# GpSimd instructions wait for the VectorE work that stands ahead of them on the shared port in the scheduler's order

## The chip, the cores and the metric

One Trainium2 chip, one of its cores. The metric is the device time of one execution in microseconds (us). The kernel before takes 637.94 us in the median of three runs (637.08 to 638.41).

## The reference

Causal attention over 4 batches and 12 heads of 448 tokens with 64 features, and behind it a feed-forward layer over all 1792 tokens:

```python
scores = scale * np.matmul(q, k.transpose(0, 1, 3, 2))
scores = np.where(mask, -1000000000.0, scores)
attn = np.exp(scores - np.max(scores, axis=-1, keepdims=True))
attn = attn / (np.sum(attn, axis=-1, keepdims=True) + 1e-09)
attn_out = np.matmul(attn, v)
x = np.ascontiguousarray(attn_out.transpose(0, 2, 1, 3)).reshape(B * S, H * D)
h = x @ w_in                              # 1792x768 by 768x2048
g = h * np.clip(h + 3.0, 0.0, 6.0) / 6.0
out = g @ w_out                           # 1792x2048 by 2048x768
```

All inputs and the output are float32.

## The kernel before

The 1792 tokens are done in four groups of 448 (`S`). Group 0 holds the first 112 rows of every batch, groups 1 to 3 the later ones, cut so that each has 448 rows. `first_pair` computes the attention of group 0 and `unit` that of groups 1 to 3, for one pair of heads at a time. `group` runs the feed-forward layer for groups 0 and 1; groups 2 and 3 share one layer (`last_x`, `last_sums`, `last_first`, `last_second`) that works on sums and differences of blocks with seven products in place of eight.

Float32 products are made of three passes on TensorE: each operand is cut into a high part, rounded to a format of fewer bits (`float32r`), and the rest, and `triple` (lines 674 to 676) multiplies high by high, high by low and low by high. The cutting is what most of the other engines' work is: ScalarE makes the high part (`move`, line 274; tiles `wh`, `gh`), and VectorE or GpSimd subtracts it (`minus`, line 286; tiles `wl`, `gl`, `kl`). The attention has besides, in `unit`: the mask and the row maximum on VectorE (line 561), the exponential on ScalarE (line 568), the inverse of the row sums on VectorE (lines 580 and 581), the scaling of the rows by it on VectorE or GpSimd (line 588; tiles `pr` of 112x224 and 112x336, and a `d` tile of 112x448), the transposes of the scaled rows on TensorE (line 600), and the product with v (line 529).

The order of the work is no fixed program. All steps are first recorded as `Op`s in a `Flow` with a key (roughly the time at which a step is due), the engines that may do it and their relative cost, and the tiles it touches. `Flow.run` then goes through them as a list scheduler with its own idea of durations, gives each to an engine and a time, and returns a list that is sorted by time. At the end of the kernel each entry is emitted in that order, so every engine gets its instructions in the scheduler's order, and the framework adds the semaphore waits that the data need.

The scheduler knows a port that VectorE and GpSimd share. Each `Op` has a set `port` (line 66): GpSimd always, and VectorE only where no tile of the `Op` lies in PSUM. In `run`, an `Op` whose engine is in its `port` does not start while `self.port`, the time until which the port is taken, lies ahead. So in the plan no VectorE `Op` of that kind and no GpSimd `Op` lie beside each other. Before the change nothing in the program holds the chip to that: each of the two engines starts an instruction as soon as its data are there. A few short VectorE steps are recorded with `port=False` (the inverse on lines 580 and 581 is one) and are outside the rule.

Of the kernel before, what the change touches and what calls it, by code (L numbers as in the profile page):

```python
# [16 lines left out]
B, H, S, D = 4, 12, 448, 64  # L17
# [51 lines left out]
class Flow:  # L69
# [119 lines left out]
    def start(self, o, e, now, need, out, busy, post):  # L189
        for t, n in need.items():  # L190
            self.free[t] -= n
        for b in o.bufs:
            b.held = True
        t, o.ends = now, []
        if e == "PE" and o.tiled != self.mode:
            t += self.SWITCH / 2
            self.mode = o.tiled
        for d, emit, _ in o.parts:
            out.append((t, len(out), e, emit))
            t += d * o.ways[e][0]  # L200
            if o.nbytes:
                self.dma = max(self.dma, t) + o.nbytes / self.DMA_RATE
                o.ends.append(self.dma + self.DMA_LATENCY)
            else:
                o.ends.append(t)
        busy[e] = t
        if e in o.port:
            self.port = t
        post(t, "idle", None)
        post(o.ends[-1], "end", o)  # L210
        for a, i in o.then:
            a.waits -= 1
            a.ready = max(a.ready, o.ends[i] + (0 if o.nbytes or e == "PE" and list(a.ways) == [e] else self.TAIL if list(a.ways) == [e] else self.LATENCY))
            if not a.waits:
                post(max(a.ready, now), "ready", a)
# [3 lines left out]
def tile_causal_attention_hardswish_moe(ctx: ExitStack, tc: tile.TileContext, q, k, v, w_in, w_out, out):  # L219
    nc = tc.nc  # L220
# [42 lines left out]
    def dma(key, nbytes, o, i, r=(), w=(), queue="SP"):  # L263
        start = nc.sync.dma_start if queue == "SP" else nc.scalar.dma_start
        flow.op(key, {queue: (1, 0)}, [(0.1, lambda e: start(out=o(), in_=i()), w)], r, nbytes=nbytes)
# [30 lines left out]
    def setup():  # L296
        nc.vector.memset(ident, 1.0)
        nc.vector.memset(mask, 0.0)
        nc.vector.memset(three, 3.0)
        nc.gpsimd.affine_select(  # L300
            out=ident, in_=ident, pattern=[[-1, C]], base=0, channel_multiplier=1,
            compare_op=ALU.is_equal, fill=0.0,
        )
        nc.gpsimd.affine_select(
            out=mask[:, R:], in_=mask[:, R:], pattern=[[-1, C]], base=0, channel_multiplier=1,
            compare_op=ALU.is_ge, fill=-8.0e9,
        )
        nc.vector.tensor_copy(identr, ident)
        nc.vector.tensor_copy(maskr, mask[:, R:].unsqueeze(1).to_broadcast([C, B, C]))
# [361 lines left out]
    def triple(ps, n, wh, wl, c, xh, xl, start, stop, more=False):  # L671

        a = slice(128 * c, 128 * c + 128)
        nc.tensor.matmul(ps, ap(wh)[:, a], xh, start=start, stop=False, skip_group_check=more)  # L674
        nc.tensor.matmul(ps, ap(wh)[:, a], xl, start=False, stop=False, skip_group_check=more)  # L675
        nc.tensor.matmul(ps, ap(wl)[:, a], xh, start=False, stop=stop, skip_group_check=more)  # L676
# [377 lines left out]
    last_second(last_first(last_x()))  # L1054
    order = flow.run()
    setup()
    with tc.manual_schedule():
        for _, _, e, emit in order:
            emit(e)


# [34 lines left out]
```

## Time and profile before

| | |
|---|---|
| median of three runs | 637.94 us (637.08 to 638.41) |
| profiled execution, its own time | 639.0 us |
| its span, first to last instruction | 637.3 us |
| mean granted TensorE clock | 0.991 |
| TensorE matmul busy | 609.3 us, 96% of the span |
| VectorE busy | 530.8 us, 83% |
| ScalarE busy | 372.1 us, 58% |
| GpSimd busy | 248.4 us, 39% |

The engines are PE (TensorE; PEld is its weight load), DVE (VectorE), ACT (ScalarE), POOL (GpSimd) and SP (the queue that issues most transfers). Of a matmul the profile shows a modelled end, and matmuls overlap. "Idle before" is the time in which an engine did nothing in front of an instruction, with what released it behind the arrow. An instruction that an engine has begun and that cannot go on, because another engine has a resource, is shown as a longer instruction and not as idle time.

### The profile page before, as it was taken

The numbers are of one execution on the slowest core, as the hardware profiler recorded it, in microseconds if no ns is written. First come the engines' busy times: TensorE is split into PE (matmuls) and PEld (weight loads), VectorE is DVE, ScalarE is ACT, GpSimd is POOL, SyncE is SP. The second block draws the span as 40 slices with busy tenths as digits, with TensorE's granted clock in tenths as the row PEclk, the third lists the DMA queues.
The fourth block names the chain that finished last, engine by engine and source line by source line (L and its number), as shares of the span: only waits on it lengthen the run. The fifth ranks groups of instructions, "written<-read, shape, count | busy, mean of one in ns | idle before, by whom it ended". The sixth has DMA issues, their size and how long they took to land. (4 is left out here: it accounts for less than half of the span.)

```text
span 637.3 us, 11372 instructions
## 1 busy us (share of the span) xinstructions
PE 609.3 (96%) x3636; PEld 529.9 (83%) x3636; DVE 530.8 (83%) x1130; ACT 372.1 (58%) x865; POOL 248.4 (39%) x248
## 2 busy tenths in 40 slices
PE   7789989999999999899998999999999999999997
PEld 5569769788778888778777888898999999999996
DVE  4799999879787889978998798389999899999561
ACT  3866656655456777567566656365545566555530
POOL 1666657455455454545555243003411045030000
PEclk9979999999999999989999999999999999999999
DMA  9978878779877865645556764445434545774421
GB/s 210 257 252 281 277 227 239 274 210 288 284 237 236 269 201 164 202 130 153 144 153 180 216 183 126 140 137 164 160 106 144 198 147 172 233 241 126 122 70 61
DMA packets 86139, 121.35 MB, mean 190 GB/s; under 512 B 22784, under 2 KB 61888, under 8 KB 86080
## 3 DMA queue, kind: packets, MB, share of 16 engines
q1 hardware_dynamic: 85648, 120.45, 62.4%
q8 instruction: 29, 0.48, 0.3%
q14 instruction: 30, 0.25, 0.1%
q10 hardware_dynamic: 432, 0.17, 0.1%
HBM read 93.45 MB, written 27.13 MB: 189 GB/s over the span
## 5 line engine op out<-in xcount | busy, mean ns | idle before, releaser
L674 PE MATMUL b<-d,wh 128*128 128x448 f32 x504 | 187.5, 372 | 1.9 <-DVE vr L286 1.6
L676 PE MATMUL b<-d,wl 128*128 128x448 f32 x504 | 183.0, 363 | 0.0
L675 PE MATMUL b<-d,wh 128*128 128x448 f32 x504 | 182.1, 361 | 0.0
L274 ACT CAST wh<-wd 128x768 fp32r<-128x768 f32 (+1 forms) x92 | 71.7, 780 | 62.5 <-PE b L675 50.8
L674 PEld LDWEIGHTS b<-d,wh 128*128 128x128 f32 x504 | 94.7, 188 | 10.6 <-DVE vr L286 2.8
L286 DVE TENSOR_TENSOR wl<-wd,wh 128x768 fp32r<-128x768 f32 (+1 forms) x79 | 76.1, 963 | 31.7 <-ACT wh L274 29.6
L676 PEld LDWEIGHTS b<-d,wl 128*128 128x128 f32 x504 | 94.6, 188 | 7.0
L675 PEld LDWEIGHTS b<-d,wh 128*128 128x128 f32 x504 | 94.6, 188 | 5.9
L561 DVE CUSTOM_DVE_ANT_0 b<-b,mask 112x448 f32<-112x448 f32 (+2 forms) x144 | 69.5, 534 | 19.2 <-PE b L506 12.6
L286 POOL TENSOR_TENSOR wl<-d,wh 128x512 fp32r<-128x512 f32 (+1 forms) x40 | 61.3, 1532 | 43.9 <-ACT wh L274 36.3
L674 PE MATMUL b<-gh,wh 128*128 128x448 f32 x192 | 73.8, 384 | 1.4 <-DVE d L277 1.1
L676 PE MATMUL b<-gh,wl 128*128 128x448 f32 x192 | 69.8, 363 | 0.0
L675 PE MATMUL b<-gl,wh 128*128 128x448 f32 x192 | 69.6, 362 | 0.0
L274 ACT COPY d<-b 112x336 f32<-112x336 f32 (+3 forms) x122 | 51.5, 452 | 28.9 <-PE b L600 23.5
L286 POOL TENSOR_TENSOR wd<-wd 128x256 f32<-128x256 f32 (+1 forms) x13 | 13.7, 1054 | 95.3 <-DVE wl L286 46.6
L568 ACT ACTIVATE pr<-b,prow 112x336 f32<-112x336 f32 (+1 forms) x96 | 46.8, 496 | 6.5 <-DVE prow L561 3.0
L600 PE MATMUL b<-ident,pr 112*112 112x112 f32 x240 | 44.1, 263 | 5.0 <-ACT pr L568 2.4
L588 POOL TENSOR_SCALAR pr<-pr,prow 112x224 f32<-112x224 f32 (+1 forms) x55 | 30.1, 558 | 47.4 <-DVE prow L581 40.5
L529 PE MATMUL b<-d,vr 112*64 112x224 f32 (+2 forms) x504 | 46.0, 334 | 0.0
L529 PEld LDWEIGHTS b<-d,vr 112*64 112x64 f32 x504 | 31.1, 139 | 15.5 <-issue 2.6
L274 ACT CAST wh<-d 128x512 fp32r<-128x512 f32 (+1 forms) x40 | 28.3, 708 | 24.5 <-DVE d L653 16.4
L568 ACT ACTIVATE d<-b,prow 112x448 f32<-112x448 f32 x48 | 30.2, 635 | 21.1 <-DVE prow L561 16.1
(115 smaller groups left out, 1191.4 us busy)
## 6 DMA issues: line engine op xcount, KB each, us to landing
wd<-in_w_in_dram SPq DMA_DIRECT2D x32, 384.0 KB, 5.6
wd<-in_w_out_dram SPq DMA_DIRECT2D x24, 512.0 KB, 5.4
wd<-kept_w SPq DMA_DIRECT2D x32, 384.0 KB, 3.7
wd<-kept_w SPq DMA_DIRECT2D x84, 128.0 KB, 3.2
d<-in_k_dram SPq DMA_DIRECT2D x80, 112.0 KB, 2.7
kept_w<-d SPq DMA_DIRECT2D x16, 384.0 KB, 6.4
kept_w<-d SPq DMA_DIRECT2D x24, 256.0 KB, 5.3
wd<-kept_w SPq DMA_DIRECT2D x24, 256.0 KB, 2.9
```

What stands on the lines that cost most here:

```text
L274: nc.scalar.copy(o(), i()) if scale is None else nc.scalar.mul(o(), i(), scale)
L286: (nc.gpsimd if e == "P" else nc.vector).tensor_tensor(o(), a(), b(), op)
L529: nc.tensor.matmul(ap(av)[64 * e:64 * e + 64, off + nq - w:off + nq], ap(vr)[:, j, e, :], ap(ph)[:, e, o:o + w], start=(j == 0), stop=(j = ...
L561: lambda _, e=e, i=i, w=w, dst=dst, st=st: nc.vector.tensor_tensor_reduce(dst(), dst(), mask[:, S - w:], -0.125, 3.0e38, ALU.add, ALU.min, ...
L568: lambda _, e=e, i=i, dst=dst, st=st, pr=pr: nc.scalar.activation(row_of(pr, e, i), dst(), ACTF.Exp, bias=ap(st)[:, e, i:i + 1], scale=-1. ...
L588: (nc.gpsimd if w == "P" else nc.vector).tensor_scalar(x, x, ap(st)[:, e, 4 + i:5 + i], 1.0, ALU.mult, ALU.mult)
L600: nc.tensor.transpose(ap(tp)[:C, C * o:C * o + C], row_of(pr, e, i)[:, C * j:C * j + C], ident)
L674: nc.tensor.matmul(ps, ap(wh)[:, a], xh, start=start, stop=False, skip_group_check=more)
L675: nc.tensor.matmul(ps, ap(wh)[:, a], xl, start=False, stop=False, skip_group_check=more)
L676: nc.tensor.matmul(ps, ap(wl)[:, a], xh, start=False, stop=stop, skip_group_check=more)
```

## The change

`Flow.start` hands each instruction's `port` on with its entry, and the loop that emits keeps the last instruction of a VectorE `Op` that uses the port (`older`). The next GpSimd instruction in the list gets a dependency on it, as though it read what that instruction writes, and `older` is cleared, so that one GpSimd instruction waits and those behind it in GpSimd's own queue come after it anyway. VectorE gets no wait on GpSimd.

```diff
-            out.append((t, len(out), e, emit))
+            out.append((t, len(out), e, emit, o.port))
...
+
+    sync = mybir.DependencyInfo(mybir.DependencyClass.Sync, mybir.DependencyReason.DATA)
+    older = None
     with tc.manual_schedule():
-        for _, _, e, emit in order:
+        for _, _, e, emit, port in order:
+            traced = nc.cur_bb.bb.instructions
+            n = len(traced)
             emit(e)
+            if e == "D" and "D" in port:
+                older = traced[-1].name
+            elif e == "P" and older:
+                tc.add_manual_dep(traced[n], older, sync, reason="port")
+                older = None
```

The plan is the same, and no engine's instructions change places. 73 of GpSimd's 242 tensor instructions get the new dependency. Where the data made such an instruction wait for VectorE already, the wait is now for a later point of VectorE's work; where not, a wait is new. In the listings below `DVE_49` and the like are the semaphores by which an engine tells how far it has come.

The first place is GpSimd's queue in group 0's feed-forward layer, where `gl` is the low part of a hidden row and `wl` that of a weight; after them stands the scaling of a short row of the next attention unit:

```order
 L286 TENSOR_TENSOR gl<-r,gh 128x448 [waits Activation_49]
 L588 TENSOR_SCALAR pr_993<-pr_993,prow 112x224 [waits DVE_49]
-L286 TENSOR_TENSOR gl<-r,gh 128x448 [waits Activation_49]
+L286 TENSOR_TENSOR gl<-r,gh 128x448 [waits DVE_49,Activation_49]
 L286 TENSOR_TENSOR wl<-d,wh 128x768 [waits PE_49,Pool_49]
 L588 TENSOR_SCALAR pr_1005<-pr_1005,prow 112x224 [waits DVE_49]
```

The second `gl` waited for ScalarE's high part alone and now waits for VectorE too; the `wl` behind it has no wait of its own for VectorE and comes after it. The same pattern stands once more, one unit later.

The second place is GpSimd's queue in group 1's feed-forward layer, two weights' low parts and the scaling of a row behind them:

```order
 L286 TENSOR_TENSOR wl<-wd,wh 128x768 [waits PE_49,Activation_49,Pool_49]
-L286 TENSOR_TENSOR wl<-wd,wh 128x768 [waits PE_49,Activation_49]
+L286 TENSOR_TENSOR wl<-wd,wh 128x768 [waits DVE_49,PE_49,Activation_49]
 L588 TENSOR_SCALAR pr_3425<-pr_3425,prow 112x224 [waits DVE_49]
 L588 TENSOR_SCALAR pr_3468<-pr_3468,prow 112x336
```

The first `wl` starts as before, the second one only after VectorE.

The third place is a little later in the same layer, where GpSimd scales two full rows:

```order
 L286 TENSOR_TENSOR wl<-wd,wh 128x768 [waits PE_49,Activation_49]
-L588 TENSOR_SCALAR d<-d,prow 112x448 x2
+L588 TENSOR_SCALAR d<-d,prow 112x448 [waits DVE_49]
+L588 TENSOR_SCALAR d<-d,prow 112x448
 L588 TENSOR_SCALAR pr_3921<-pr_3921,prow 112x224 [waits DVE_49,Activation_49]
```

The first of the two rows now waits for VectorE, where before it came straight behind the `wl`.

## Rows read from the trace of the kernel before

**Rows 1.** Windows: length, busy of PE, PEld, DVE, ACT, POOL, PEclk, DMA, GB/s.

```profile
210.00:425.00 215.00, 206.81 (x1372) 178.39 (x1371) 179.93 (x428) 138.69 (x346) 89.88 (x101) 0.99 0.58 169
425.00:637.30 212.30, 206.88 (x1030) 192.31 (x1028) 177.46 (x287) 107.67 (x181) 39.14 (x29) 1.00 0.48 150
```

**Rows 2.** TensorE's waits from 45 us on: us in total, times, longest us.

```profile
PE b L600 <- DVE d L588: 3.9, 5, 1.5
PE b L600 <- ACT pr L568: 2.4, 2, 1.8
PE b L674 <- DVE vr L286: 1.6, 2, 1.5
PE b L600 <- POOL pr L588: 1.5, 1, 1.5
PE b L508 <- DVE d L286: 1.3, 4, 0.5
PE b L674 <- DVE d L277: 1.1, 1, 1.1
PE b L600 <- DVE pr L588: 1.0, 1, 1.0
```

**Rows 3.** Line 588 on VectorE, full rows: ns min/median/max, first and last start.

```profile
L588 DVE TENSOR_SCALAR d<-d,prow x30: 433/446/2048, 52.8 to 394.9; 112x448 f32<-112x448 f32 x30
```

**Rows 4.** Timeline, 82 to 90 us, GpSimd, VectorE, TensorE: start, us, engine, instruction [idle before <-releaser].

```profile
82.65 1.22 POOL L286 TENSOR_TENSOR gl<-r,gh 128x448 fp32r<-128x448 f32 x1 [0.58 <-ACT gh L274]
83.82 1.95 POOL L286 TENSOR_TENSOR wl<-d,wh 128x768 fp32r<-128x768 f32 x1
89.18 0.88 POOL L588 TENSOR_SCALAR pr<-pr,prow 112x224 f32<-112x224 f32 x2 [3.41 <-DVE prow L581]
...
82.53 1.52 DVE L588 TENSOR_SCALAR pr<-pr,prow 112x224 f32<-112x224 f32 x2
83.97 2.05 DVE L588 TENSOR_SCALAR d<-d,prow 112x448 f32<-112x448 f32 x1
...
86.08 0.31 PE L600 MATMUL b<-ident,d 112*112 112x112 f32 x1 [0.25 <-DVE d L588]
89.68 0.41 PE L600 MATMUL b<-ident,pr 112*112 112x112 f32 x2 [1.50 <-POOL pr L588]
```

**Rows 5.** Timeline, 110 to 114 us, the same three engines.

```profile
111.17 1.91 POOL L286 TENSOR_TENSOR wl<-d,wh 128x768 fp32r<-128x768 f32 x1
...
111.32 2.01 DVE L588 TENSOR_SCALAR d<-d,prow 112x448 f32<-112x448 f32 x1
...
113.39 0.31 PE L600 MATMUL b<-ident,d 112*112 112x112 f32 x1 [1.38 <-DVE d L588]
```

**Rows 6.** Timeline, 263 to 270 us, the same.

```profile
267.78 1.81 POOL L286 TENSOR_TENSOR wl<-wd,wh 128x768 fp32r<-128x768 f32 x1 [2.69 <-ACT wh L274]
...
263.55 1.57 DVE L580 TENSOR_SCALAR prow<-prow 112x4 f32<-112x4 f32 x1
...
267.85 2.00 DVE L588 TENSOR_SCALAR d<-d,prow 112x448 f32<-112x448 f32 x1
...
269.90 0.31 PE L600 MATMUL b<-ident,d 112*112 112x112 f32 x1 [1.54 <-DVE d L588]
```

**Rows 7.** Timeline, 301 to 304 us, the same.

```profile
301.65 2.21 POOL L588 TENSOR_SCALAR d<-d,prow 112x448 f32<-112x448 f32 x2
...
302.73 0.70 DVE L286 TENSOR_TENSOR d<-d 64x112 fp32r<-64x112 f32 x2
...
303.30 0.45 PE L600 MATMUL b<-ident,d 112*112 112x112 f32 x3
```

**Rows 8.** Timeline, 568 to 596 us: GpSimd, VectorE, ScalarE.

```profile
568.49 1.81 POOL L286 TENSOR_TENSOR gh<-gl,gh 128x448 f32<-128x448 f32 x1 [3.57 <-DVE gh L286]
...
578.34 1.15 DVE L286 TENSOR_TENSOR gh<-gl,gh 128x448 f32<-128x448 f32 x2
...
594.50 1.03 ACT L274 CAST d<-gh 128x448 fp32r<-128x448 f32 x2
```

## The prediction

> **What bounds the kernel now.** Start with the windows by stage: from 210 us to the end TensorE is busy for 206.81 of 215.00 and 206.88 of 212.30 us, VectorE for 179.93 and 177.46, GpSimd for 89.88 and 39.14 [rows 1]. TensorE sets the time, and the most that a change on other engines can return is TensorE's idle time. Next, what ends that idle time. From 45 us on, the list of TensorE's waits has seven entries of 1.0 us or more, in sum 12.8 us [rows 2]. Four of them (3.9, 1.5, 1.3 and 1.0) end on an instruction of VectorE or GpSimd that works between tiles in SBUF and so counts as a user of the shared port in the scheduler; `vr` (1.6) and the copy of line 277 (1.1) read a PSUM bank, and 2.4 us end on ScalarE. About 13 us is the ceiling for this change, and the 7.7 us of the four are what it acts on directly.
>
> Then the form of those instructions. The scaling of a full row on VectorE takes 433 ns at least and 446 in the median of 30, but 2048 at most [rows 3]. The timeline shows what lies beside the long ones. At 83.97 us it takes 2.05 us while GpSimd has a `wl` of 1.95 us, begun 0.15 us before [rows 4]; at 111.32 us 2.01 us beside a `wl` begun 0.15 us before [rows 5]; at 267.85 us 2.00 us beside one begun 0.07 us before [rows 6]. Each ends about 0.25 us after GpSimd's, so nearly all of its own 0.44 us is done once GpSimd has let go: one engine has the port and the other stands. The Trainium skill (SBUF — State Buffer, the section on the two separate sides) calls the pair of ports an exclusive lock that whichever of the two starts first holds for its whole instruction; these three rows agree.
>
> **What the change adds.** It moves nothing on any engine and removes nothing. 73 GpSimd instructions get a dependency on VectorE. Laid against the trace (start of each, against the end of the VectorE instruction that it is to wait for), 14 started after that end anyway and 59 started before it: 5 before 210 us, 33 from there to 425, 21 behind. Their lateness is 136 us in sum, from 0.02 to 11.0 us; the longest is the `gh` at 568.49 us, which is to wait for the second of the two at 578.34 [rows 8]. What is paid in GpSimd's time is no path by itself: it is idle for 125 us in the one stage and 173 in the other [rows 1]. A wait that now ends on VectorE costs about 0.1 us more by itself (TensorE started 0.05 us after the VectorE instruction that released it [rows 6]); 59 of these are 6 us of that idle time. No SP transfer is moved; some wait for a buffer that GpSimd frees later.
>
> **The terms.** First, group 0's layer. With the change the `gl` at 82.65 and the `wl` at 83.82 stand back until the VectorE rows are done. These are two short rows, together 1.52 us where 0.33 us each would do without GpSimd, so 0.9 too long, and the full row, 1.6 us too long [rows 4]. VectorE is 2.5 us earlier. TensorE's 0.25 us at 86.08 go, and at 89.68 so do the 1.50 us in front of a row that GpSimd scales: it had waited 3.41 us for the inverse, which stands in VectorE's queue behind the long rows [rows 4]. **−1.75 us.**
>
> Second, the same one unit later: 1.38 us in front of 113.39 go [rows 5]. **−1.4 us.** Third, group 1: the `wl` at 267.78 will wait for two more pairs of scaled rows, the full row ends at 268.3 instead of 269.85, and 1.54 us in front of 269.90 go [rows 6]. **−1.5 us.** The condition is the same in all three: what GpSimd makes there must have slack. The low parts `wl` and `gl` are made for products that the plan has ahead, and neither stands in TensorE's list as a wait on GpSimd [rows 2]; the one with the longest lateness, 11.0 us, is ready at 570.30 and read by ScalarE in the pair at 594.50 [rows 8]. I take it that the others have slack too, the more so as VectorE ends earlier than in the old trace.
>
> Fourth, the small ones: the rest of the first line (3.9 − 0.25 − 1.38 − 1.54 = 0.7 us) and the four waits of the score products for a `d` of line 286 (1.3 us) [rows 2]. Not each has a GpSimd instruction beside it that the change moves; between 0 and −2.0 I take −1.3.
>
> Fifth, the waits that end on ScalarE, on the copies and on `vr` (2.4, 1.1, 1.6) and the one for `pr` (1.0) [rows 2], 6.1 us. Those end on work that stands behind VectorE's queue, so a freer VectorE may shorten them; but behind them may be a transfer or TensorE itself. Between 0 and −6.1 I take −1.6, a quarter, nearer to the lower end, because none of the first three is a user of the port itself.
>
> Sixth, a loss that can be read off: at 301.65 GpSimd scales two full rows in 2.21 us and TensorE takes the first at 303.30 without idle time [rows 7]. With the change the first waits for the last of the VectorE pair that now ends at 303.43. Two instructions of about 0.65 us in place of the 2.21 end at 304.1 for the first, so TensorE is up to 0.8 us late, less what VectorE gains there: **+0.6 us**.
>
> Sum: −1.75 − 1.4 − 1.5 − 1.3 − 1.6 + 0.6 = −6.95, rounded to −7.0 us. The profiled execution took 639.0 us, 1.1 above the median of 637.94; it becomes 632.0, and the median **631.0 us**.
>
> **A rule against it.** The rows say that a GpSimd instruction that waits for the port loses nothing that TensorE needs. If the port is simply an exclusive lock, what one engine gains the other loses, and the sum of both stays. The Trainium skill has the exclusive lock (the section named above) and advises in Perfetto Trace Analysis (on the GPSIMD instruction) to treat a GpSimd span in a profile as unreliable. By these the order would be worth nothing of its own, and my reading of who held the port would be soft: that is the first rival below, 637.5 us. What speaks against it is VectorE's own rows: 2.05 for 0.44 us, three times, each with TensorE idle behind it [rows 4 to 6].
>
> **The rivals.** (a) *The wait only changes hands.* VectorE is faster, but TensorE's idle time is then ended by ScalarE, a transfer, or a GpSimd row, in the same places. For it: 2.4 us already end on ScalarE [rows 2]. Against it: the three big terms are waits for exactly the stretched row. It gives 0 to −1.3 us: 637.5 us. That the new waits are held already by other semaphores, so that the program does the same, falls here too; the listings show new ones at all three places. (b) *Half of it*: the three big terms come, the rest is paid back by GpSimd rows that are late: −2 to −3.5 us, about 635. (c) *Slower*: in group 1's stage, 33 GpSimd starts move back, and among these are the low parts `kl` of keys and the scaled rows, whose readers, score products and transposes, stand close behind. The place is the sixth term; its price is 0.6 to 0.8 us each. It decides when more than one in three of the 33 is late for TensorE: 14 of them at 0.75 us are +10, which with −7 makes +3: 641 us. Against it: VectorE ends earlier there, and TensorE's list has a single entry on GpSimd so far [rows 2].
>
> **The numbers.** My forecast has 0.68 (628 to 634), half of it 0.12, no gain 0.10, slower 0.10. By 0.2% (1.3 us), about what a measurement can tell from no change: faster 0.80, same 0.10, slower 0.10. The low end takes most of the fifth term's 6.1 and the fourth's 2.0 without the sixth: −4.65 − 2.0 − 4.3 = −11, 627 us; the high end takes in half the gain and part of the first rival: 637. By one case alone it would be 628 to 634.
>
> **What would show it.** Right: no full row of line 588 on VectorE above about 1 us in groups 0 and 1; the entry for `d` of line 588 in TensorE's list down from 3.9 to below 1.0; GpSimd's idle time ended far more often by VectorE. The inverse on line 580 stays stretched in places (1.57 us at 263.55 [rows 6]), since the scheduler does not count it as a user of the port. Wrong: new entries in TensorE's list on GpSimd's `kl`, `wl` or `pr` of more than 2 us in sum, or `d` of line 588 still at 3 us with another instruction beside it.

## The result and the profile after

The changed kernel takes 628.46 us in the median of 4 runs (627.74 to 628.89), the kernel before 638.17 on the same chip (637.08 to 638.47): a ratio of 0.985 [0.9833, 0.9867], or −9.7 us. The forecast was 631.0 with a range of 627 to 637, and faster. The sign, the range and the mechanism hold; the size was 2.7 us short.

The profiled execution took 628.89 us, 10.1 less than the one of before. The head of its page, with the span and each engine's busy time:

```profile
span 627.2 us, 11383 instructions
...
PE 604.6 (96%) x3636; PEld 530.0 (85%) x3636; DVE 515.1 (82%) x1130; ACT 373.1 (59%) x865; POOL 234.4 (37%) x248
```

VectorE was busy for 530.8 us before and GpSimd for 248.4. **Both are shorter**, by 15.7 and 14.0 us, with the same count of instructions. An instruction that stands at the shared port counts as busy, so the page of before held these waits as work. GpSimd now waits on a semaphore instead, which the profile shows as idle time. TensorE's waits from 45 us on (us in total, times, longest), which answer to [rows 2]:

```profile
PE b L600 <- ACT pr L568: 4.3, 2, 3.7
PE b L600 <- DVE pr L588: 0.8, 1, 0.8
PE b L600 <- POOL d L588: 0.5, 1, 0.5
PE b L674 <- DVE d L653: 0.3, 1, 0.3
PE b L508 <- ACT d L274: 0.2, 1, 0.2
```

Five of the seven entries are gone, all but the two for `pr` that end on ScalarE and VectorE: the 3.9 us for `d` of line 588, 1.6 for `vr`, 1.5 for GpSimd's `pr`, 1.3 for `d` of line 286, and 1.1 for the copy of line 277. One has grown, that on ScalarE, from 2.4 to 4.3 us. The two groups of VectorE's lines (ns least, median, longest), the first of which answers to [rows 3]:

```profile
L588 DVE TENSOR_SCALAR d<-d,prow x30: 434/445/664, 52.5 to 386.6; 112x448 f32<-112x448 f32 x30
L580 DVE TENSOR_SCALAR prow<-prow x36: 158/286/1833, 46.7 to 383.4; 112x6 f32<-112x6 f32 x12, 112x2 f32<-112x2 f32 x12, 112x4 f32<-112x4 f32 x12
```

The longest full row took 2048 ns and now takes 664. The inverse on line 580, which the scheduler does not count as a user of the port, is stretched more than before. Of the kernel before:

```profile
L580 DVE TENSOR_SCALAR prow<-prow x36: 152/165/1572, 47.0 to 391.9; 112x6 f32<-112x6 f32 x12, 112x2 f32<-112x2 f32 x12, 112x4 f32<-112x4 f32 x12
```

Group 0's layer, which answers to [rows 4] (start, us, engine, instruction, idle time before it and its end):

```profile
82.72 0.44 DVE L588 TENSOR_SCALAR d<-d,prow 112x448 f32<-112x448 f32 x1
...
83.31 1.15 POOL L286 TENSOR_TENSOR gl<-r,gh 128x448 fp32r<-128x448 f32 x1 [1.61 <-PE b L600]
...
84.41 1.86 POOL L286 TENSOR_TENSOR wl<-d,wh 128x768 fp32r<-128x768 f32 x1
...
86.61 0.89 POOL L588 TENSOR_SCALAR pr<-pr,prow 112x224 f32<-112x224 f32 x2 [0.33 <-DVE prow L581]
...
85.11 0.35 PE L600 MATMUL b<-ident,pr 112*112 112x112 f32 x2
85.31 0.26 PE L600 MATMUL b<-ident,d 112*112 112x112 f32 x1
...
87.21 0.35 PE L600 MATMUL b<-ident,pr 112*112 112x112 f32 x2
```

GpSimd's `gl` starts 0.15 us after the full row has ended at 83.16, and the `wl` comes behind it. The full row takes 0.44 us where it took 2.05, and neither of TensorE's rows at 85.31 and 87.21 has idle time before it. (The releaser named for `gl` is the event that came last by the profile; the semaphore that the change added is VectorE's.) The second and the third place, which answer to [rows 5] and [rows 6], look the same:

```profile
107.90 0.44 DVE L588 TENSOR_SCALAR d<-d,prow 112x448 f32<-112x448 f32 x1
...
109.59 1.86 POOL L286 TENSOR_TENSOR wl<-d,wh 128x768 fp32r<-128x768 f32 x1
...
262.26 0.44 DVE L588 TENSOR_SCALAR d<-d,prow 112x448 f32<-112x448 f32 x1
...
263.54 1.83 POOL L286 TENSOR_TENSOR wl<-wd,wh 128x768 fp32r<-128x768 f32 x1 [1.99 <-DVE d L588]
```

And the place of the forecast loss, which answers to [rows 7]:

```profile
293.01 1.25 POOL L588 TENSOR_SCALAR d<-d,prow 112x448 f32<-112x448 f32 x2 [1.61 <-DVE d L286]
...
293.71 0.60 PE L600 MATMUL b<-ident,d 112*112 112x112 f32 x4 [0.48 <-POOL d L588]
```

The two rows take 1.25 us together, not 2.21, but start only once VectorE's pair is done, and TensorE waits 0.48 us for the first.

**Where the time went.** Both kernels give TensorE the same instructions in the same order, so the start of each can be subtracted. These are all the steps of 0.3 us and more behind 45 us (start before, start after, line, shift of the row ahead and of this row):

```
 86.08  85.31 L600  -0.36 ->  -0.77   term 1
 89.68  87.21 L600  -0.81 ->  -2.47   term 1
113.39 109.31 L600  -2.54 ->  -4.08   term 2
180.93 176.42 L600  -4.13 ->  -4.51
226.12 220.98 L508  -4.74 ->  -5.13   term 4
269.90 262.76 L600  -5.59 ->  -7.14   term 3
270.81 to 274.11    -7.15 ->  -8.77   steps of 0.1 and 0.2 (clock)
279.37 269.95 L508  -8.76 ->  -9.43   term 4
303.30 293.71 L600 -10.23 ->  -9.59   term 6
307.44 297.20 L600  -9.54 -> -10.25   term 4
333.38 321.31 L674 -10.76 -> -12.08   term 5, copy
339.62 329.42 L600 -12.12 -> -10.21   term 5, ScalarE
339.62 to 342.38   -10.21 ->  -7.83   steps of 0.1 to 0.2 (clock)
350.82 342.45 L508  -7.78 ->  -8.37   term 4
443.42 433.33 L674  -8.46 -> -10.09   term 5, vr
456.48 445.93 L674 -10.21 -> -10.55   term 5, vr
the end                      -10.49
```

The rest is steps under 0.3 us. Two stretches are no wait at all: TensorE's granted clock differs there. Windows of the kernel before, then of the new one (length; busy us of PE, PEld, DVE, ACT, POOL; granted clock; DMA share; GB/s):

```profile
268.00:272.00 4.00, 2.38 (x16) 1.94 (x18) 3.61 (x6) 1.74 (x5) 1.59 (x1) 0.83 0.70 203
272.00:274.20 2.20, 2.20 (x14) 1.44 (x16) 1.24 (x5) 0.45 (x2) 1.75 (x4) 0.54 0.00 0
```

```profile
325.00:329.40 4.40, 0.69 (x5) 0.39 (x4) 1.57 (x8) 2.16 (x6) 2.70 (x4) 0.82 0.94 297
329.40:334.50 5.10, 5.08 (x19) 4.66 (x20) 3.65 (x7) 4.10 (x14) 1.88 (x2) 0.50 0.41 116
334.50:340.00 5.50, 5.50 (x46) 4.18 (x46) 3.14 (x8) 1.71 (x5) 0.84 (x1) 0.99 0.31 83
```

In the old kernel TensorE waited 0.98 us in front of 268.08 and 1.54 in front of 269.90, and then had a granted clock of 0.54 over 2.2 us, close to the lower of its two levels (1.2 and 2.4 GHz). In the new one the second wait is gone and the clock there is 1.00, which is worth 1.6 us that no list of waits shows. (Whether that clock hangs on the wait is asked in the first two experiments.) At 325 us the new kernel has the reverse: a wait of 3.72 us, then 5.1 us at 0.50 with TensorE busy throughout, which give back 2.4 us on top of the wait. Where that wait comes from, in the old kernel (two lines) and in the new one (three; SPq is the queue that issues transfers):

```profile
337.45 0.57 ACT L274 CAST d<-d 128x448 fp32r<-128x448 f32 x1 [2.21 <-DMA d<-kept_x]
...
339.62 0.31 PE L600 MATMUL b<-ident,pr 112*112 112x112 f32 x1 [1.81 <-ACT pr L568]
```

```profile
322.25 0.89 SPq L265 DMA_DIRECT2D d<-kept_x  x2
...
327.24 0.56 ACT L274 CAST d<-d 128x448 fp32r<-128x448 f32 x1 [4.67 <-DMA d<-kept_x]
...
329.42 0.43 PE L600 MATMUL b<-ident,pr 112*112 112x112 f32 x1 [3.72 <-ACT pr L568]
```

ScalarE's cast of a tile loaded from `kept_x` stands ahead of the `pr` that TensorE needs. The load is issued 10.5 us earlier than in the old kernel (332.75 there), but ScalarE comes to its cast 12.6 us earlier (its instruction ahead starts at 322.13, not 334.77). VectorE's gain has run into a transfer.

### The profile page after: what moved, and what is told of

Its sections match the earlier page's. It is cut to its first block, busy times and chain, and to the rows that moved or that the text cites. A ratio compares the mean times of both kernels' runs of the same rounds, so it can differ in the third digit from the quotient of the medians.

```text
span 627.2 us, 11383 instructions
## 1 busy us (share of the span) xinstructions
PE 604.6 (96%) x3636; PEld 530.0 (85%) x3636; DVE 515.1 (82%) x1130; ACT 373.1 (59%) x865; POOL 234.4 (37%) x248
## 5 line engine op out<-in xcount | busy, mean ns | idle before, releaser
L286 POOL TENSOR_TENSOR wd<-wd 128x256 f32<-128x256 f32 (+1 forms) x13 | 11.3, 869 | 97.4 <-DVE d L286 39.1
L588 POOL TENSOR_SCALAR pr<-pr,prow 112x224 f32<-112x224 f32 (+1 forms) x55 | 28.5, 528 | 42.1 <-DVE prow L581 22.7
L674 PEld LDWEIGHTS b<-gh,wh 128*128 128x128 f32 x192 | 36.5, 190 | 5.0 <-issue 1.2
```

Source lines behind the costliest of these rows:

```text
L286: (nc.gpsimd if e == "P" else nc.vector).tensor_tensor(o(), a(), b(), op)
L588: (nc.gpsimd if w == "P" else nc.vector).tensor_scalar(x, x, ap(st)[:, e, 4 + i:5 + i], 1.0, ALU.mult, ALU.mult)
```

## The experiments

Theory: VectorE's instructions that TensorE waits for stood at the port behind GpSimd work that had slack; putting that work behind VectorE removes the wait, place by place. The rivals are the three of the prediction. Each ratio is against the kernel before on the same chip. All edits are in the loop that emits the order, unless said. None leaves out work.

**One wait alone, in group 0.** The `gl` at 82.65 is GpSimd's instruction 40:

```diff
-            elif e == "P" and older:
-                tc.add_manual_dep(traced[n], older, sync, reason="port")
+            elif e == "P":
+                if older and pool == 40:
+                    tc.add_manual_dep(traced[n], older, sync, reason="port")
                 older = None
+                pool += 1
```

> One single wait of the 73: the low part gl that starts at 82.65 us in the trace of the kernel before. Theory: the 0.25 and 1.50 us of TensorE's idle time at 86.08 and 89.68 us go, in starts 2.0 us, and stay gone to the end: -1.7 to -2.1 us. Rival (early time is lost again before the end): -0.5 us or less.

Measured: 636.52 us against 639.12, a ratio of 0.9959 [0.9935, 0.9982]. GpSimd's rows of this kernel at the place:

```profile
82.08 1.15 POOL L286 TENSOR_TENSOR gl<-r,gh 128x448 fp32r<-128x448 f32 x1 [1.61 <-PE b L600]
83.19 1.86 POOL L286 TENSOR_TENSOR wl<-d,wh 128x768 fp32r<-128x768 f32 x1
85.38 0.88 POOL L588 TENSOR_SCALAR pr<-pr,prow 112x224 f32<-112x224 f32 x2 [0.33 <-DVE prow L581]
```

GpSimd's scaled rows wait 0.33 us for the inverse where they waited 3.41 [rows 4], and TensorE's shift goes from −1.59 to −3.71 from 86.08 to 89.68, with no step of 0.3 us and more behind it. (The −1.59 is a difference in the first 45 us, which vary by that much from one execution to the next.) One semaphore of 73 is worth what the first term says. The interval reaches from −1.2 to −4.2 us, so the size rests on the trace.

In steps under 0.3 us this execution gains 1.6 us more, and not by its one semaphore: in group 1 it still has the waits of 0.98 and 1.54 us, but the clock behind them is 1.00, where the kernel before has 0.83 and 0.54. The second wait and the window from it:

```profile
266.12 0.31 PE L600 MATMUL b<-ident,d 112*112 112x112 f32 x1 [1.54 <-DVE d L588]
```

```profile
266.12:270.40 4.28, 4.28 (x43) 3.50 (x44) 3.06 (x8) 2.21 (x6) 2.06 (x4) 1.00 0.38 126
```

**One wait alone, in group 1.** The same with `pool == 147`, the `wl` at 267.78.

> One single wait of the 73: the low part wl that starts at 267.78 us in the trace of the kernel before. Theory with TensorE's clock: the 1.54 us of idle time at 269.90 go, and the half clock behind it (granted 0.54 from 272.0 to 274.2 us, 1.0 us, and some of the 0.83 before it) goes too: -2.3 to -3.2 us, with no stretch below 0.9 between 268 and 276 us. Rival (idle time alone, the clock falls all the same): -1.5 us.

Measured: 637.23 us, 0.9971 [0.9953, 0.9989]. In the trace TensorE's shift goes from −0.89 to −2.43 at 269.90, and the shift at the end is −3.9, so this execution gains 3.0 us there and not 1.5. The other half is the clock; its window at the place:

```profile
268.00:272.00 4.00, 4.00 (x42) 3.15 (x41) 3.16 (x8) 2.46 (x7) 3.41 (x4) 1.00 0.68 177
```

It has 1.00 and 42 matmuls where the kernel before has 0.83 and 16. But the execution of the experiment above had a clock of 1.00 here with the wait still in place. Of the 13 profiled executions of this document six have the wait of 1.54 us, and the clock falls behind it in five; seven do not have it, and it falls in none. So the 1.55 us of the wait are shown, and that the 1.6 us of the clock belong to it is likely but not shown: the times alone do not tell −1.5 from −3.0.

**The waits in three parts by time.** As above with `pool < 113` (9 waits, to 210 us), `113 <= pool < 213` (43, to 425 us) and `pool >= 213` (21).

> The waits are kept for the 113 GpSimd instructions of the first 210 us alone (9 of the 73 waits). Theory (VectorE's scaled rows no longer stand behind a GpSimd instruction there, TensorE gets them earlier): TensorE is 4.5 us ahead at 210 us in the trace of the changed kernel, and this kernel keeps 3.5 to 4.5 us of it to the end, about -4.0 us. Rival 1 (an early gain is eaten by later waits that are not TensorE's, such as a transfer): -1 us or less. Rival 2 (the whole gain needs the later waits too, early ones only shift work): 0.

> The waits are kept for the 100 GpSimd instructions between 210 and 425 us alone (43 of the 73). Theory: in the changed kernel's trace TensorE gains 6 to 7.6 us between 210 and 330 us and gives 3.6 us back at 330 us in a longer wait for ScalarE and at a lower clock behind it; alone, -4 us, with -2 if the give-back is as long here and -6 if it is not. Rival (GpSimd's late low parts cost TensorE as much as VectorE's rows gain): 0 to +3 us.

> The waits are kept for the last 29 GpSimd instructions alone, behind 425 us (21 of the 73). Theory: only the wait for vr at 443 us and its small neighbour can go: -1.5 to -2 us. Rival (late low parts and sums of GpSimd reach TensorE, the longest is held back 11 us): 0 to +2 us.

Measured against 639.47: 635.15 us, 0.994 [0.9921, 0.996]; 634.08, 0.9918 [0.9893, 0.9942]; 638.3, 0.9988 [0.997, 1.0007]. The three gains are 0.6, 0.8 and 0.1%, together 1.5%, as much as the whole change: within their intervals the parts add up. The last third can't be told from none by its time. In its trace TensorE's wait for `vr` falls from 1.6 to 0.5 us, and behind 425 us its shift has steps of −1.64 at 443.42, −0.34 at 456.48 and +0.64 at 469.20.

**Only the waits behind a scaled row.** Instructions of line 588 get a mark "S", and of the 73 waits only the 20 are kept in which the VectorE instruction ahead has it:

```diff
             if e == "D" and "D" in port:
                 older = traced[-1].name
+                scaled = "S" in port
             elif e == "P" and older:
-                tc.add_manual_dep(traced[n], older, sync, reason="port")
+                if scaled:
+                    tc.add_manual_dep(traced[n], older, sync, reason="port")
```

> A GpSimd instruction waits only where the VectorE instruction ahead of it is one that scales a row (line 588): 20 of the 73 waits, 9 before 210 us and 11 from there to 425. Theory (what TensorE waited for was the stretched scaled row): the early gain of 4 us and the entry for d of line 588 in the later part, 2 us, come with it, -5 to -6.5 us; the four short waits of the score products (1.3 us) and vr (1.6 us) stay. Rival (the gain is spread over all of VectorE's queue, by its 50 us of stretched time as a whole): 20 of 73 waits give a quarter, -2.5 us.

Measured: 633.87 us against 639.3, 0.992 [0.9898, 0.9942]. About a quarter of the waits gives half of the gain. TensorE's entry for `d` of the scaling falls to 0.7 us, while `vr` stays (1.9 us) and `pr` from ScalarE grows (3.4).

**The order reversed.** VectorE's port users wait for the GpSimd instruction ahead of them:

```diff
-            if e == "D" and "D" in port:
+            if e == "P":
                 older = traced[-1].name
-            elif e == "P" and older:
+            elif e == "D" and "D" in port and older:
```

> The order is held the other way round: each VectorE instruction that uses the port waits until the GpSimd instruction that stands ahead of it in the scheduler's order has ended; GpSimd waits for nothing new. Theory (the gain comes from who is held back, since GpSimd has slack and VectorE has none): no gain, VectorE idles behind GpSimd, +3 to +15 us. Rival (the gain comes from following the plan at all, or from the two never meeting at the port): -4 to -10 us, like the change.

Measured: 644.94 us, 1.0099 [1.0067, 1.0131], slower by 5.5 us in the medians. The same port users are tied together, but the waits are on the other side. Of this kernel, one entry of TensorE's waits, then two of VectorE's:

```profile
PE b L600 <- DVE pr L588: 5.2, 5, 1.8
```

```profile
DVE pr L588 <- POOL pr L588: 3.2, 5, 1.5
DVE pr L588 <- POOL wl L286: 2.1, 1, 2.1
```

The entry on VectorE's `pr` was 1.0 us before [rows 2]. The old meetings stay as well, since nothing holds a GpSimd instruction that comes early: the longest full row of line 588 takes 1996 ns. A dependency between the two engines thus doesn't pay by itself; it pays where it holds back the one that has slack.

**GpSimd behind any VectorE instruction**, users of the port or not:

```diff
-            if e == "D" and "D" in port:
+            if e == "D":
```

> A GpSimd instruction waits for whatever VectorE instruction stands ahead of it in the scheduler's order, also those that read or write PSUM and don't use the port: about as long an order, more lateness, no more port freed. Theory (GpSimd has slack, the port alone is what is won): within 2 us of the change, 628 to 631 us. Rival (GpSimd's slack is already used up by the change, so that more lateness reaches TensorE): 633 us or more.

Measured: 641.33 us, 1.0035 [1.002, 1.005], slower by 2.0 us. My expectation fell and the rival's held: GpSimd's slack runs out. Of this kernel's list of TensorE's waits:

```profile
PE b L600 <- POOL pr L588: 3.1, 3, 1.3
...
PE b L600 <- POOL d L588: 1.2, 1, 1.2
```

The change has one entry of 0.5 us on GpSimd. The rule that decides which VectorE instructions count is a part of the gain.

**The inverse counted too.** The operations with no port set (line 580's kind) also hold GpSimd back:

```diff
-            if e == "D" and "D" in port:
+            if e == "D" and ("D" in port or not port):
```

> The short VectorE steps that the scheduler leaves out of the port's rule (the inverse on lines 580 and 581, the two of the first pairs) count too, so that GpSimd waits for them as well. In the changed kernel's trace line 580 is too long in 17 places, by 11 us in sum, up to 1.67 us. Theory (a stretched step costs only where TensorE waits for what stands behind it): no entry of TensorE's list there ends on the inverse, so 0 to -1.5 us against the change, 627 to 628.5 us. Rival (freed time of VectorE is worth time as such): -3 us or more, 625.5 us or less.

Measured: 628.89 us against 639.3, 0.984 [0.9819, 0.9861], no different from the change's 0.985. Line 580 still took 1755 ns at most and 212 in the median, against 286 in the change: the edit removed only a part of what it was to remove. That the inverse's stretch costs nothing is therefore not shown.

**The cast of `kept_x` later on ScalarE.** Nothing is moved but one cast and its low part on GpSimd, to where the next cast of the kind stands, nine ScalarE instructions on. First in the kernel before, without any port wait, then in the changed kernel (where the operation's number is field 5):

```diff
-            out.append((t, len(out), e, emit))
+            out.append((t, len(out), e, emit, o.key[1]))
...
+    late = [x for x in order if x[4] in (2256, 2257)]
+    order = [x for x in order if x[4] not in (2256, 2257)]
+    at = next(i for i, x in enumerate(order) if x[4] == 2258)
+    order[at:at] = late
```

> The kernel before with the cast of ScalarE and its low part nine instructions later, and no wait on the port at all. Theory (the transfer's wait is a second limit, which mostly bites once the port's stalls are gone): in the trace of the kernel before ScalarE idles 2.21 us in front of this cast and TensorE 1.81 us behind it at full clock, so -1 to -2 us, less than the 4 us it gave on top of the change. Rival (the two are independent): -4 us.

> The change, and one cast of ScalarE (a high part of the last layer's x, read first at 415 us) with its low part on GpSimd stands nine instructions later in the order. In the changed kernel's trace it is at the head of ScalarE's queue from 322.6 to 327.2 us and waits there 4.67 us for its transfer, with the exponentials behind it, for which TensorE waits 3.7 us at 329.4; TensorE's clock is at 0.50 for the next 5.1 us. Theory (the change's gain past 320 us is held up by that transfer): -3 to -5.5 us against the change, 623 to 625.5 us. Rival (the exponentials wait for their scores, or the transfer load holds everything there): 627 us or more.

Measured: alone 636.3 us against 639.12, 0.9958 [0.9942, 0.9974]; with the change **624.49 us** against 639.3, 0.9786 [0.9753, 0.982], 4.4 below the kernel of the experiment above on the same chip. This beats both kernels. One entry of TensorE's waits and the window at the place, in the changed kernel with the cast moved:

```profile
PE b L600 <- ACT pr L568: 0.6, 1, 0.6
```

```profile
325.00:331.00 6.00, 5.92 (x39) 5.34 (x38) 5.78 (x17) 5.64 (x18) 4.34 (x6) 1.00 0.94 280
```

The wait of 3.7 us is gone and the clock stays at 1.00. The profiled executions are 13.9 us (both edits), 10.1 (the change) and 1.6 (the cast) below that of the kernel before: by them the cast is worth 3.8 us on top of the change and 1.6 without it. By the medians it is 4.4 and 2.8, the second more than the −1 to −2 that I expected, and as one of the four runs with both edits took 629.18 us, the times do not show that the two differ. That the change had made this cast dearer rests on the traces: the wait at this row falls by 3.6 us there, with the lower clock behind it, and by 1.6 here.

## Why the prediction was right, and where it was short

**Terms 1 to 3** (−1.75, −1.4, −1.5) came as −2.1, −1.5 and −1.55 in the table of steps. The single waits show that the first and the third are due to the GpSimd instruction that the prediction names; the second has no run of its own, and its step is −1.55 with the first third of the waits alone. The condition, that the low parts have slack, held: TensorE's list has no entry on `wl` or `gl`. The longest lateness, the `gh` behind [rows 8], is now an idle time of 13.7 us on GpSimd that nobody waits for.

**Term 4** (−1.3) was undersized. The four steps that the table names are −2.4 us, and no entry for `d` of line 588 or of line 286 is left. Among the steps under 0.3 us, eight at the score products (lines 508 and 509) give another 1.1, and one gives 0.15 back. I had doubted that each small wait would go. The four did, wholly, and they were 0.16, 0.45, 0.56 and 0.44 us of idle time, 1.6 in sum; the rest of the 2.4 is the next point.

**What most terms had too small** is the price of a wait: I took TensorE's idle time for the whole of it. The profile counts idle time from the shown end of the matmul ahead, and without a wait the next matmul starts before that end, as in the new rows of group 0: the pair begun at 85.11 ends at 85.46, and the next starts at 85.31. Twelve rows of the table lose their idle time wholly. It was 9.2 us, and their steps are 11.2: at eleven of them 0.15 to 0.23 us more than was shown as idle, at 269.90 no more. So the list of waits is no ceiling either, as the prediction has it with its 13 us.

**Term 5** (−1.6 for 6.1 us) has the right sum for the wrong reason. I sized it by the form of the instruction waited for: the copy and `vr` read PSUM and are no users of the port, so I took a quarter. But what counts is the instruction ahead in VectorE's queue. Of the kernel before:

```profile
439.16 1.86 POOL L286 TENSOR_TENSOR wl<-wd,wh 128x768 fp32r<-128x768 f32 x1 [0.26 <-ACT wh L274]
...
439.24 2.20 DVE L286 TENSOR_TENSOR pr<-wd,pr 128x384 fp32r<-128x384 f32 x1
...
443.42 0.47 PE L674 MATMUL b<-d,wh 128*128 128x448 f32 x1 [1.47 <-DVE vr L286]
```

The `pr` took 2.20 us beside a `wl`, where it takes 0.55 in the new trace; three instructions behind it stands the `vr` that TensorE waits for. The copy of line 277 stood some places behind two scaled rows of 3.84 us (shown below). So both entries went wholly: −1.3 and −2.0 (two steps of `vr`), not a quarter. Against that the wait on ScalarE grew by 1.9. With these two errors the term's waits come to −1.4.

**Term 6** (+0.6) came as +0.64, at the row forecast.

**The step that was mis-sized** is thus term 4, "between 0 and −2.0 I take −1.3": by its four steps it is −2.4, and with the eight small ones −3.5; the 2.0 us beyond the shown idle time are the greater part of what the sum lacks. The six terms come to −8.3 by the named steps (−2.1 − 1.5 − 1.55 − 2.4 − 1.4 + 0.64) against −6.95. The step at 180.93 gives another 0.4 and the ones under 0.3 us 2.2, the eight among them. The sum also lacks a kind of term: it has waits only, and no TensorE clock, which gave 1.6 us at 270 to 274 and took 2.4 at 339 to 342, 0.8 lost in all. From −0.36 to −10.49 that makes the −10.1 of the profiled executions.

**Rival (a)**, that the wait only changes hands, falls for the whole and holds at one place. As a whole both engines are shorter. At 325 us a transfer takes over, which is its mechanism, and with the clock it costs 4.3 us there. The reading that GpSimd's spans are not to be relied on did not matter here: a `wl` takes 1.86, 1.86 and 1.83 us in the rows above, and the single waits moved what those rows said they would. **Rival (b)**, half of it paid back by GpSimd, falls: GpSimd's entries on TensorE's list went from 1.5 to 0.5 us. **Rival (c)**, slower, falls for this change, but its mechanism is real: it is what GpSimd behind any VectorE instruction does.

Of the signs named beforehand, the full row's longest (0.66 us), the entry for `d` (gone) and the inverse that stays stretched came true, and so did the one on GpSimd's idle time: VectorE ends it 61 times, 214 us in sum, where it was 37 times and 134 us. None of the signs of being wrong came.

## What to carry to other kernels

Where VectorE and GpSimd meet, look for a VectorE row far above the median of its form, and at what stands beside it on GpSimd; the wait that it causes may be named after an instruction several places behind it. If GpSimd has slack there and VectorE's reader has none, a semaphore that puts GpSimd second gives back most of what the reader waited for (here 1.5%, where the reverse lost 1.0%). After such a gain, look for the engine that now arrives too early at a transfer, and move that instruction behind what is needed at once.

## What was not expected of the hardware

**Who gets the port.** Of the kernel before, GpSimd and VectorE around 327 us:

```profile
326.80 1.35 POOL L281 TENSOR_SCALAR d<-d 128x784 fp32r<-128x784 f32 x1
328.13 0.65 POOL L588 TENSOR_SCALAR d<-d,prow 112x448 f32<-112x448 f32 x1
328.75 1.14 POOL L286 TENSOR_TENSOR d<-d 128x448 fp32r<-128x448 f32 x1
329.85 1.16 POOL L286 TENSOR_TENSOR kl<-d 128x448 fp32r<-128x448 f32 x1
...
326.83 0.61 DVE L286 TENSOR_TENSOR gl<-r,gh 128x448 fp32r<-128x448 f32 x1
327.36 3.84 DVE L588 TENSOR_SCALAR pr<-pr,prow 112x224 f32<-112x224 f32 x2
```

VectorE's two scaled rows take 0.64 us in the new trace. Here they took 3.84, most of it the second:

```profile
328.20 3.00 DVE L588 TENSOR_SCALAR pr<-pr,prow 112x336 f32<-112x336 f32 x1
```

It ended 0.2 us after the last of three GpSimd instructions that came one behind the other: VectorE did not get in between them. Just before, it was the other way round. GpSimd's row began 0.03 us ahead of VectorE's `gl`, yet the `gl` kept its 0.61 us and GpSimd took 1.35 for what takes 0.84 in the new trace. The Trainium skill (SBUF — State Buffer, the section on the two separate sides) gives the pair to whichever starts first, for its whole instruction. GpSimd's row at 328.13, 0.07 us ahead of VectorE's at 328.20, agrees. By the profile's starts its next two, at 328.75 and 329.85, do not, for VectorE's row had begun ahead of both, and neither does the `gl`. So "first" is not always read off the start of a row.

**It is the port, and not GpSimd's running as such.** VectorE's mask and row maximum have a tile in PSUM and so are no users of the port by the scheduler's rule. In the kernel before:

```profile
L561 DVE CUSTOM_DVE_ANT_0 b<-b,mask x144: 392/546/667, 40.8 to 387.2; 112x448 f32<-112x448 f32 x48, 112x336 f32<-112x336 f32 x48, 112x224 f32<-112x224 f32 x48
```

Of these 144 rows 101 lie beside a GpSimd instruction for more than 0.1 us, and none is stretched: those of 112x448 take 0.61 to 0.67 us beside one and 0.62 to 0.67 without.

**Size does not protect.** The first step of the inverse, on line 580, has 112x2 to 112x6 elements and takes 0.16 us alone, but up to 1.83; that one, of the new kernel, ended 0.02 us after the second of two GpSimd instructions. The second step, on line 581, has the same elements and no tile in PSUM either, and took 0.19 us at most in both kernels, beside GpSimd too.

**The clock after a wait.** A wait of 3.72 us was followed by 5.1 us at a granted clock of 0.50, and two of 0.98 and 1.54 us by 2.2 us at 0.54. The same two were followed by a clock of 1.00 in the kernel with one wait in group 0, and at the same place as the first, a wait of 1.81 us in the kernel before and one of 3.1 us in the kernel with the middle third of the waits were followed by a clock of 1.00. So a wait on TensorE cost its length in some of these executions and some 1.6 times that in others (3.72 and 2.4 us more; 2.5 and 1.6 more). What decides it was not tried.
